# A two-layer linear-attention and routed-FFN kernel: the reciprocal denominators reach all features through DRAM instead of a TensorE broadcast, with fewer two-column matmuls and another order of instructions

## Chip, cores and metric

The kernel runs on one core of one Trainium2 chip. Its time is the device time of one execution in microseconds; the number quoted is the median of several runs. Besides the runs there is one profiled execution, and every duration below that is read from a view is from that one.

The five engines are called by their short names: PE is TensorE (PEld its weight loads), DVE is VectorE, ACT is ScalarE, POOL is GpSimd, SP is SyncE, which only issues DMAs here.

## What is computed

One token matrix x (2048 tokens, 512 features, bf16) passes four residual steps: attention A, routed FFN B, A again, B again, each on a layer-normalised x. The weights are the same in both rounds.

```
A: q, k, v = layernorm(x) @ wqkv            # 32 heads of 16 features
   pq, pk = phi(q), phi(k)                  # phi(t) = (t+1 if t>0 else exp(t)) + 1e-6
   kv = sum over tokens of pk^T v           # 16 x 16 per head
   z  = sum over tokens of pk               # 16 per head
   o  = (pq @ kv) / (pq . z + 1e-6)         # one denominator per token and head
   x  = x + o @ wo
B: r = layernorm(x) @ w_r; pick the one token with the largest r
   y = (silu(xs @ w_gate) * (xs @ w_up)) @ w_down * sigmoid(r)   # for this token alone
   x = x + layernorm(x); the picked token also gets + y
```

So there are 2048 x 32 denominators per layer, and each is needed on the 16 features of its head.

## The kernel before, in words

**Layout.** x lies in SBUF as 16 tiles of 128 tokens (`x_tok`), the normalised x both so (`xn_tok`) and transposed with features on partitions (`xnT`, one buffer per layer). Features come in four chunks m of 128, tokens for q and for the denominators in four groups tg of 512.

**Stages of a layer.** `kv_tile` computes keys and values of a token tile (four accumulating 128x512 matmuls each; L591, or L601 where a value tile carries router columns) and adds the tile's pk^T v, with a column of ones for z, into two PSUM banks reserved for it (L620). `q_group` computes the transposed queries of 512 tokens, one bank for each chunk (L681). Both apply phi in three steps on three engines: ACT takes exp from PSUM into a ring buffer `Eb` (L527), POOL clips it at 1 (L529), DVE combines it with the matmul's result (L531); only then is the bank free. `kv_out` then folds the per-head kv into wo: Mw = kv @ wo, four 128x512 matrices (L658), evicted on ACT and DVE (L663, L666).

**The division.** `den_group` handles 512 tokens. Four matmuls with z as weights (L779) give the denominators, one partition for each 4 features, so 32 partitions for each chunk, 128 in all; a head's value is there four times. ACT takes 1/d as exp(-ln(d)) into `rden` (L784, L786). To bring the value from 32 partitions to the 128 of its chunk, four matmuls with a 0/1 matrix `sel` (L809) copy it into four PSUM banks, and four DVE instructions multiply `pqT` in place by them (L814). `out_tile` then computes pq @ Mw for a token tile (L836; six tiles of layer 1 add x by an identity matmul, L839), DVE adds the residual and sums the row (L859), ACT squares and sums (L865).

**Narrow matmuls.** The router value r is linear in x, so it is built from its parts rather than from the new x: a matmul of only 2 columns with the same weights follows its wide one (`mm_keep`, L519: it reuses the loaded weights). The 2 columns are the high and low bf16 half of a vector. They go along with the output tiles of both layers (128 of them), with the layer-0 value tiles 4 to 15 (48) and the Mw products (8); for tiles 0 to 3 they stand alone (L754, 16).

**Between the layers.** `ln_mid` forms the statistics of both normalisations for groups of 2 or 4 tiles, POOL normalises (L718) and SP issues a DMA transpose for each tile (L409). Router and FFN of the first B run amid the keys and values of layer 1: layer 1 computes k and v for x without the picked token's y, and `coupling` repairs that by a rank-2 correction (L1094, L1114), a patch of one `xnT` column and of one x row on POOL (`x_patch`, L1136). `x2_explicit` (L931) updates six x tiles on POOL. At the end `final_group` normalises for the output (L1172, L1176) and SP stores it; the second B runs as a serial tail, with the token's column gathered through a register-held index (L975).

**Order.** Every operation is added once to a list with its reads and writes; ORDER, a list of operation numbers written out in the file, fixes the sequence for each engine, SP's DMA issues among them, and BANKS the PSUM bank of each buffer: six banks (0 to 5) serve everything but the kv sums. Engines run their sequence in order; semaphores are derived from reads and writes, and a buffer that takes over a bank waits for all users of the one before. All DMAs of SP go through one queue.

Of the kernel before, what the change touches and what calls it, by code (L numbers as in the profile page):

```python
# [7 lines left out]
ALU = mybir.AluOpType  # L8
# [3 lines left out]
P = 128  # L12
S_TOK = 2048
# [12 lines left out]
0 11 30 1 58 15 2 16 25 17 36 7 54 14 26 29 24 23 35 37 27 3 56 4 13 21 22 19 18 32 28 31 20 55 10 33 12 34 5  # L26
51 67 6 53 8 60 57 9 68 61 69 62 59 70 63 71 52 64 65 72 66 88 73 152 86 76 159 153 74 154 77 87 160 89 163 75
97 78 90 161 155 79 156 91 164 83 92 80 84 157 41 162 93 81 85 158 38 165 82 94 177 98 95 39 99 166 42 40 178
96 43 100 44 45 101 173 167 102 272 103 168 174 46 170 169 104 184 171 110 106 105 180 108 185 175 111 109 191
119 107 181 176 112 182 172 113 192 187 120 114 143 115 179 183 188 194 117 116 130 189 186 121 195 284 118  # L30
190 196 198 122 47 123 124 201 199 125 197 126 193 202 205 131 132 128 127 144 133 219 141 134 203 206 48 135
129 212 220 136 200 204 221 213 223 137 142 222 145 207 146 355 49 230 224 139 147 138 50 273 150 208 226 231
140 148 237 227 214 149 209 228 233 215 238 274 229 216 151 234 275 235 247 217 236 296 248 210 249 336 244
337 250 211 334 320 245 333 218 332 240 335 225 241 251 242 232 252 261 243 288 285 262 286 239 289 304 263
287 290 246 264 305 258 291 297 306 253 259 280 298 307 321 299 254 281 322 265 282 323 255 283 256 276 266
257 268 277 260 278 269 292 279 270 316 293 271 267 294 317 328 339 338 295 318 358 329 341 422 359 319 300
330 423 356 340 331 324 360 357 424 361 325 365 301 326 362 308 302 363 312 303 309 327 342 310 313 364 516
343 314 311 517 348 346 315 344 349 350 347 345 469 352 351 470 425 353 354 471 427 375 518 428 372 426 376
366 418 373 377 369 367 399 374 429 368 395 370 472 401 396 378 439 474 402 371 400 473 403 430 404 475 405
# [38 lines left out]

class Op:
    __slots__ = ("idx", "eng", "fn", "est", "prio", "deps", "is_dma", "nbytes", "kind", "sem", "val", "pos",  # L80
                 "has_dependents", "name", "banks", "known", "waits", "occ", "pre", "pre_deps")


class Sched:
# [1231 lines left out]
```

## Time and profile before

| what | value |
|---|---|
| median of 3 runs | 173.48 us (173.47 to 174.39) |
| the profiled execution | 172.91 us |
| its span, first to last instruction | 170.7 us |
| busy PE / DVE / ACT / POOL | 155.0 / 130.3 / 113.7 / 72.8 us |
| instructions in the span | 3500 |
| DMA | 15.80 MB in 23183 packets |
| granted TensorE clock | full up to 158 us, about half in the tail |

Rows are of four kinds. In the windows view a row is a stretch of time: busy time and number of instructions of PE, PEld, DVE, ACT and POOL, then the granted clock, the DMA engines' share and GB/s. In the groups, a row is a source line, engine, operation, output and inputs with shapes and count; then the busy time in us, the mean ns of one, and the idle time of the engine before them with what ended it. In the timeline a row is a start, a duration, an engine and an operation, merged when alike; the bracket is the engine's idle time before it and what ended that. In the DMA issues the last number is the median time from issue to landing. Consecutive instructions of PE and of DVE overlap in their rows, so a group's busy time is more than the engine's time for it: start-to-start distances tell that.

### The profile page before, as it was taken

The numbers are of one execution on the slowest core, as the hardware profiler recorded it, in microseconds if no ns is written. First come the engines' busy times: TensorE is split into PE (matmuls) and PEld (weight loads), VectorE is DVE, ScalarE is ACT, GpSimd is POOL, SyncE is SP. The second block draws the span as 40 slices with busy tenths as digits, with TensorE's granted clock in tenths as the row PEclk, the third lists the DMA queues.
The fourth block names the chain that finished last, engine by engine and source line by source line (L and its number), as shares of the span: only waits on it lengthen the run. The fifth ranks groups of instructions, "written<-read, shape, count | busy, mean of one in ns | idle before, by whom it ended". The sixth has DMA issues, their size and how long they took to land.

```text
span 170.7 us, 3500 instructions
## 1 busy us (share of the span) xinstructions
PE 155.0 (91%) x1332; PEld 73.0 (43%) x1148; DVE 130.3 (76%) x426; ACT 113.7 (67%) x293; POOL 72.8 (43%) x123
## 2 busy tenths in 40 slices
PE   7889999999999778999999898999999898997184
PEld 2335344445544222433344365667444233332073
DVE  6698998351669899999999662254698999999921
ACT  3476557744867786789779461764678669888920
POOL 4043776931655410242694689240576320153000
PEclk9999999999999999999999999999999999999855
DMA  5999433349995000033055430000000000031430
GB/s 133 344 312 255 83 75 62 63 70 340 352 381 213 4 0 0 0 61 67 0 103 109 95 67 0 4 0 4 0 2 0 0 4 0 0 123 61 184 127 0
DMA packets 23183, 15.80 MB, mean 93 GB/s; under 512 B 15616, under 2 KB 21632, under 8 KB 23040
## 3 DMA queue, kind: packets, MB, share of 16 engines
q1 hardware_dynamic: 23168, 15.60, 32.6%
q8 instruction: 9, 0.15, 0.4%
q14 instruction: 6, 0.05, 0.1%
HBM read 9.83 MB, written 2.10 MB: 70 GB/s over the span
## 4 chain that ended last, share of the span: by engine, by line
PE 58%; DVE 28%; DMA 6%; POOL 2%; ACT 2%; issue 1%; SPq 0%
PE ps L591 17%; PE ps L681 13%; PE ps L836 9%; DVE pqT L814 7%; PE ps L601 7%; DVE x_tok L859 5%; PE ps L620 4%; DMA x_tok<-in_A_x_dram 4%; DVE pqT L531 3%; DMA xnT<-xn_tok 3%; PE ps L1021 3%; DVE pk L531 2%; DVE st L725 2%; PE ps L1047 2%; DVE xn_tok L1176 1%
## 5 line engine op out<-in xcount | busy, mean ns | idle before, releaser
L529 POOL TENSOR_SCALAR Eb<-Eb 128x512 bf16<-128x512 bf16 x64 | 38.9, 612 | 45.7 <-ACT Eb L527 38.2
L591 PE MATMUL ps<-wqkv,xnT 128*128 128x512 bf16 x208 | 50.0, 379 | 1.2 <-DVE pk L531 0.5
L527 ACT ACTIVATE Eb<-ps 128x512 bf16<-128x512 f32 x64 | 37.6, 596 | 19.9 <-PE ps L591 9.9
L836 PE MATMUL ps<-Mw,pqT 128*128 128x512 bf16 x128 | 32.7, 377 | 1.5 <-DVE pqT L814 0.6
L681 PE MATMUL ps<-xnT,wqkv 128*128 128x512 bf16 x128 | 30.6, 380 | 1.3 <-DVE pqT L814 0.8
L531 DVE SCALAR_TENSOR_TENSOR pk<-ps,Eb 128x512 bf16<-128x512 f32 x32 | 21.6, 683 | 12.3 <-POOL Eb L529 12.3
L591 PEld LDWEIGHTS ps<-wqkv,xnT 128*128 128x128 bf16 x208 | 18.2, 97 | 21.6 <-DVE pk L531 0.9
L610 ACT ACTIVATE va<-ps 128x512 bf16<-128x512 f32 x32 | 18.8, 595 | 12.4 <-PE ps L519 4.3
L531 DVE SCALAR_TENSOR_TENSOR pqT<-ps,Eb 128x512 bf16<-128x512 f32 x32 | 21.2, 686 | 5.4 <-POOL Eb L529 5.2
L836 PEld LDWEIGHTS ps<-Mw,pqT 128*128 128x128 bf16 x128 | 12.3, 96 | 21.4 <-issue 1.8
L519 PE MATMUL ps<-mr_hl,pqT 128*128 128x2 bf16 x128 | 21.1, 165 | 0.0
L814 DVE TENSOR_TENSOR pqT<-pqT,ps 128x512 bf16<-128x512 bf16 x32 | 20.1, 682 | 0.7 <-PE ps L809 0.6
L865 ACT ACTIVATE junk<-x_tok 128x512 bf16<-128x512 bf16 x26 | 16.1, 620 | 4.2 <-DVE x_tok L859 3.9
L718 POOL TENSOR_SCALAR xn_tok<-x_tok,stat,nms 128x512 bf16<-128x512 bf16 x16 | 12.1, 768 | 15.3 <-DVE nms L901 11.3
L681 PEld LDWEIGHTS ps<-xnT,wqkv 128*128 128x128 bf16 x128 | 11.5, 97 | 15.2 <-DVE pqT L814 1.4
L601 PE MATMUL ps<-wqkv,xnT 128*128 128x512 bf16 x48 | 13.2, 377 | 0.3 <-DMA xnT<-xn_tok 0.3
L620 PE MATMUL ps<-va,pk 128*128 128x129 bf16 x128 | 12.0, 221 | 0.0
L725 DVE BATCH_NORM_STATS2 st<-x_tok 128x6 f32<-128x512 bf16 x16 | 10.3, 675 | 1.6 <-DMA x_tok<-in_A_x_dram 1.6
L859 DVE SCALAR_TENSOR_TENSOR x_tok<-x_tok,ps 128x512 bf16<-128x512 bf16 x16 | 10.7, 680 | 0.3 <-PE ps L519 0.2
L620 PEld LDWEIGHTS ps<-va,pk 128*128 128x128 bf16 x128 | 9.0, 99 | 4.6
L718 POOL TENSOR_SCALAR xn_tok<-x_tok,rs,nms 128x512 bf16<-128x512 bf16 x12 | 9.6, 806 | 2.2 <-DVE nms L738 1.9
L1176 POOL TENSOR_SCALAR xn_tok<-x_tok,us,stat 128x512 bf16<-128x512 bf16 x6 | 4.6, 774 | 13.6 <-DVE rt L1158 10.9
(207 smaller groups left out, 205.7 us busy)
## 6 DMA issues: line engine op xcount, KB each, us to landing
out_dram<-xn_tok SPq DMA_DIRECT2D x8, 256.0 KB, 2.1
wu<-in_B_w_up_dram SPq DMA_DIRECT2D x2, 896.0 KB, 9.4
wd<-in_B_w_down_dram SPq DMA_DIRECT2D x2, 896.0 KB, 9.6
wg<-in_B_w_gate_dram SPq DMA_DIRECT2D x2, 896.0 KB, 11.1
wqkv<-in_A_wqkv_dram SPq DMA_DIRECT2D x3, 512.0 KB, 7.1
x_tok<-in_A_x_dram SPq DMA_DIRECT2D x1, 1024.0 KB, 11.8
x_tok<-in_A_x_dram SPq DMA_DIRECT2D x2, 256.0 KB, 4.8
x_tok<-in_A_x_dram SPq DMA_DIRECT2D x1, 512.0 KB, 6.1
```

Of the source, the lines that this page charges most:

```text
L519: ins = e.matmul(out_ap, lhsT, rhs, start=start, stop=stop, skip_group_check=True).ins
L527: A("act", lambda e: e.activation(Eb[:, i, :], src(), ACTF.Exp), reads=[b, "table"], writes=[f"E{i}"], est=600, name=name + "E")
L529: A("pool", lambda e: e.tensor_scalar(Eb[:, i, :], Eb[:, i, :], 1.0, 0.0, op0=ALU.min, op1=ALU.max), reads=[f"E{i}"], writes=[f"E{i}"], es ...
L531: return A("dve", lambda e: e.scalar_tensor_tensor(out=dst, in0=src(), scalar=1e-6, in1=Eb[:, i, :], op0=ALU.max, op1=ALU.add), reads=[b, ...
L591: ins = e.matmul(B(b), xT[:, c, t * P:(t + 1) * P], wqkv[:, c, lo:lo + D], start=(c == 0), stop=(c == NC_D - 1))
L601: e.matmul(B(vb), xT[:, c, t * P:(t + 1) * P], wqkv[:, c, 2 * D:3 * D], start=(c == 0), stop=(c == NC_D - 1))
L620: ins = e.matmul(views[m], pk[:, i, m * P:(m + 1) * P], va[:, i, m * 129:(m + 1) * 129], start=(first and m in (0, 3)), stop=False, skip_g ...
L681: ins = e.matmul(B(qb), wqkv[:, c, qc * P:(qc + 1) * P], xnT[L][:, c, tg * 512:(tg + 1) * 512], start=(c == 0), stop=(c == NC_D - 1))
L718: A("pool", lambda e: e.tensor_scalar(xn_tok[:, t, :], x_tok[:, t, :], scale[:, t:t + 1], nbias[:, t:t + 1], op0=ALU.mult, op1=ALU.add), r ...
L814: A("dve", (lambda e, m=m, bb=bb: e.tensor_tensor(pqT[:, m, cols], pqT[:, m, cols], B(bb), ALU.mult)), reads=[bb, f"pq{tg}_{m}"], writes=[ ...
L836: e.matmul(B(ob), w, Mw[:, m, :], start=(m == 0), stop=(m == NC_D - 1 and not xb))
L859: A("dve", lambda e: e.scalar_tensor_tensor(out=x_tok[:, t, :], in0=x_tok[:, t, :], scalar=scal, in1=B(ob), op0=ALU.mult, op1=ALU.add, acc ...
```

## The change

- **Denominators.** For all eight groups, `den_group` no longer uses the `sel` matmuls. SP writes `rden` to a DRAM buffer, each of its 128 rows four times (512 rows of 1 KB, 512 KB), and after that has landed reads it back with the 512 rows as features (`rb_sb`, two buffers). DVE multiplies per token tile, all four chunks in one instruction of 128 x 512 bf16 with both inputs in SBUF; four such per group as before.
- **Router columns.** For tiles 0 to 7 the router's 2-column matmuls of layer 0 (value tiles 4 to 7, the lone ones of tiles 0 to 3, output tiles 0 to 7) are dropped. In their place 2-column matmuls follow layer 1's value matmuls of these tiles, into one bank held from the first to the reduction `Mrtx`; `router_mid` scales it.
- **kv banks.** The four kv products lie two and two in their banks, not three and one.
- **First router.** The picked row is copied on POOL (`B0xg`) and gathered from there; the statistics are summed by a matmul over all 4 x 16 columns and one reduction (as bf16 halves, in the second router in fp32). In the second router TensorE loads the index register when the index is there, and its matmuls wait for the rest; the sum `B1tot` stands ahead of the gather. `index` takes register values without another copy.
- **Rank-2 rows.** Key and value rows are computed in half-rows of 256, on four groups of columns.
- **Order.** ORDER and BANKS are new throughout. On SP: the loads of x, wk and wr come first, the weight loads for B stand between the transposes of tiles 15, 14 and 13; the new DMAs stand, in layer 0, as write 0, write 1, read 0, write 2, read 1, read 2, write 3, transposes of tiles 2 and 3, read 3; in layer 1 as write 0, write 1, read 0, read 1, write 2, write 3, read 2, read 3. On PE, in both layers the q matmuls of groups 2 and 3 stand behind the first denominators and ahead of the first output tile.

The diff, cut to its core:

```diff
-604 524 581 491 421 596 398 448 587 417 492 467 582 449 597 493 450 494 451 584 583 495 588 452 496 525 530
...
+249 289 254 294 276 243 255 295 25 250 256 281 290 257 282 264 291 285 335 336 283 296 355 286 284 301 356 292
...
+        RD = ()
+        RT = tuple(range(8))
+        RM = tuple(t for t in range(4, NT) if t not in RD + RT)
+        RS = tuple(t for t in range(4) if t not in RD + RT)
...
+        def index(e, reg, n):
+            return nc.s_assert_within(e.snap(reg, donate=True), 0, n - 1,
+                                      skip_runtime_bounds_check_because="built from max_index results alone")
...
-            if L == 0 and t in RM:
+            if L == 1 and t in RT:
+                if "b" not in rtb:
+                    rtb["b"] = bank()
+                rb = rtb["b"]
+
+                def vmr(e):
+                    ins = None
+                    for c in range(NC_D):
+                        e.matmul(B(vb), xT[:, c, t * P:(t + 1) * P], wqkv[:, c, 2 * D:3 * D], start=(c == 0),
+                                 stop=(c == NC_D - 1))
+                        ins = mm_keep(e, B(rb)[:, 2 * t:2 * t + 2], xT[:, c, t * P:(t + 1) * P], wrc_hl[:, c, :],
+                                      c == 0, c == NC_D - 1)
+                    return ins
+                A("pe", vmr, reads=[f"T{L}_{t}", "wv", "wrc_h", "wrc_l"], writes=[vb, f"rx{t}"], hold=[rb],
+                  est=864 + KEEP, name=f"A{L}v{t}")
+            elif L == 0 and t in RM:
...
-        DMAB = ()
+        DMAB = ((0, 0), (0, 1), (0, 2), (0, 3), (1, 0), (1, 1), (1, 2), (1, 3))
+        rd_dram = [nc.dram_tensor(f"rd_scr{i}", [NC_D * P, 512], BF).ap() for i in range(len(DMAB))]
 
         def den_group(L, tg):
             db = bank()
...
               reads=[f"lden{j}"], writes=[f"rden{j}"], est=629, name=f"A{L}rden{tg}")
             if (L, tg) in DMAB:
                 i = dctr[1] % 2
+                scr_d = rd_dram[dctr[1]]
                 dctr[1] += 1
-                row = 2 * NC_D * 512
-                for m in range(NC_D):
-                    src = bass.AP(rden, 32 * m * 1024 + j * 512, [[1024, 32], [0, 4], [1, 512]])
-                    dst = bass.AP(rb_sb, (i * NC_D + m) * 512, [[4 * row, 32], [row, 4], [1, 512]])
-                    DMA("sp", dst, src, [f"rb{i}_{m}"], TB * 1.25, f"A{L}rb{tg}_{m}", reads=[f"rden{j}"])
-                for m in range(0, NC_D, 2):
-                    pr = slice(m, m + 2)
-                    A("dve", (lambda e, pr=pr: e.tensor_tensor(pqT[:, pr, cols], pqT[:, pr, cols], rb_sb[:, i, pr, :],
-                                                               ALU.mult)),
-                      reads=[f"rb{i}_{m}", f"rb{i}_{m + 1}", f"pq{tg}_{m}", f"pq{tg}_{m + 1}"],
-                      writes=[f"pq{tg}_{m}", f"pq{tg}_{m + 1}"], est=690, name=f"A{L}qd{tg}_{m}")
+                DMA("sp", scr_d.rearrange("(q s) n -> q s n", s=4), rden[:, j, :].unsqueeze(1).to_broadcast([P, 4, 512]),
+                    [f"rd{L}{tg}"], 4 * TB, f"A{L}rw{tg}", reads=[f"rden{j}"])
+                DMA("sp", rb_sb[:, i, :, :], scr_d.rearrange("(m p) n -> p m n", p=P), [f"rb{i}"], 4 * TB,
+                    f"A{L}rb{tg}", reads=[f"rd{L}{tg}"])
+                for t in range(4 * tg, 4 * tg + 4):
+                    tc = slice(t * P, (t + 1) * P)
+                    rc = slice((t - 4 * tg) * P, (t - 4 * tg + 1) * P)
+                    A("dve", (lambda e, tc=tc, rc=rc: e.tensor_tensor(pqT[:, :, tc], pqT[:, :, tc], rb_sb[:, i, :, rc],
+                                                                      ALU.mult)),
+                      reads=[f"rb{i}"] + [f"pq{tg}_{m}" for m in range(NC_D)], writes=[f"pqd{t}"], est=420,
+                      name=f"A{L}qd{t}t")
                 return
...
-            if (L, k) not in rbanks:
+            keep = L == 1 or t not in RT
+            if keep and (L, k) not in rbanks:
                 rbanks[(L, k)] = bank() if L == 0 else bank(("ka", "kb")[[g[0] for g in FG].index(k) % 2])
-            rb = rbanks[(L, k)]
+            rb = rbanks[(L, k)] if keep else None
             q = t - k
 
             def womm(e):
                 ins = None
                 for m in range(NC_D):
                     w = pqT[:, m, t * P:(t + 1) * P]
-                    e.matmul(B(ob), w, Mw[:, m, :], start=(m == 0), stop=(m == NC_D - 1 and not xb))
-                    ins = mm_keep(e, B(rb)[:, 2 * q:2 * q + 2], w, mr_hl[:, m, :], m == 0, m == NC_D - 1)
+                    ins = e.matmul(B(ob), w, Mw[:, m, :], start=(m == 0), stop=(m == NC_D - 1 and not xb))
+                    if keep:
+                        ins = mm_keep(e, B(rb)[:, 2 * q:2 * q + 2], w, mr_hl[:, m, :], m == 0, m == NC_D - 1)
                 if xb:
...
+            if (L, tg) in DMAB:
+                pqr = pqr + [f"pqd{t}"]
...
+            if k in RT:
+                tiny_act(ics[:, sl], l2[:, sl], ACTF.Exp, [f"l2_{k}"], [f"ics{k}"], f"Mic{k}", scale=0.5)
+            else:
+                router_mid(ts)
+
+        def router_mid(ts):
+            sl = slice(ts[0], ts[-1] + 1)
+            k = ts[0]
+            n = len(ts)
+            u_ = usx[:, sl] if set(ts) & set(XB) else us1[:, sl]
+            if k in RT:
+                tt(rt[:, sl], rt[:, sl], ics[:, sl], ALU.mult, [f"rt{k}", f"ics{k}"], [f"rt{k}"], f"Mro{k}")
+            else:
+                rb = rbanks[(0, k)]
+                A("dve", lambda e: e.tensor_reduce(
+                    rt[:, sl], B(rb)[:, 0:2 * n].rearrange("p (m k) -> p m k", k=2), AX.X, ALU.add),
+                  reads=[f"rr0_{t}" for t in ts], writes=[f"rt{k}"], hold=[rb], est=160, name=f"Mrt{k}")
+                tt(rt[:, sl], rt[:, sl], aw[:, sl], ALU.add, [f"rt{k}"] + [f"aw{t}" for t in ts], [f"rt{k}"], f"Mro{k}")
             tt(r_bf[:, sl], rt[:, sl], rs1[:, sl], ALU.mult, [f"rt{k}", f"rs1_{k}"], [f"r{k}"], f"rbf0_{k}")
...
             gb = bank()
 
+            gregs = {}
+            if L == 0:
+                def load_t(e):
+                    e.reg_load(reg_t, idxu[0:1, 1:2])
+                    regs["t"] = index(e, reg_t, NT)
+                    return e.tensor_copy(xg[:], x_tok[:, bass.ds(regs["t"], 1), :].rearrange("p a d -> p (a d)"))
+                A("pool", load_t, reads=["idxu1"] + [f"x{t}" for t in range(NT)], writes=["xg", "regt"], est=1250,
+                  name="B0xg")
+
+            def gather_reg(e):
+                e.reg_load(reg_pe, idxu[0:1, 1:2])
+                gregs["t"] = index(e, reg_pe, NT)
+
             def gather(e):
-                e.reg_load(reg_pe, idxu[0:1, 1:2])
-                tv = e.snap(reg_pe)
                 ins = None
                 for c in range(NC_D):
-                    ins = e.matmul(B(gb)[:, c:c + 1],
-                                   x_tok[:, bass.ds(tv, 1), c * P:(c + 1) * P].rearrange("p a d -> p (a d)"),
-                                   ohp_bf[:, 0:1], start=True, stop=True)
+                    src = xg[:, c * P:(c + 1) * P] if L == 0 else x_tok[
+                        :, bass.ds(gregs["t"], 1), c * P:(c + 1) * P].rearrange("p a d -> p (a d)")
+                    ins = e.matmul(B(gb)[:, c:c + 1], src, ohp_bf[:, 0:1], start=True, stop=True)
                 return ins
-            A("pe", gather, reads=["idxu1", "ohp_bf"] + [f"x{t}" for t in range(NT)], writes=[gb], est=650,
...
-                                       start=True, stop=True),
-              reads=["part_h", "part_l", "ones_bf", "part0"], writes=[tb], est=30, name=tag + "tot")
...
+            else:
+                A("pe", lambda e: e.matmul(B(tb)[:, 0:nw], ones_mat[:, :], pv, start=True, stop=True),
+                  reads=["prod16", "ones_mat"], writes=[tb], est=280, name=tag + "tot")
+                tv_ = lambda: B(tb)[:, 0:nw].rearrange("p (k t) -> p k t", t=NT)
+                ax = AX.X
+            small(lambda e: e.tensor_reduce(tots[:, 0:nr], tv_(), ax, ALU.add), [tb], ["tots"], tag + "tots",
...
+            HD = D // 2
+
             def rows(e):
                 ins = None
                 for c in range(NC_D):
-                    for r, lo in ((0, D), (32, 2 * D)):
-                        ins = e.matmul(B(kb2)[r:r + 2, :], xcol2[:, c, :], wqkv[:, c, lo:lo + D], start=(c == 0),
+                    for r, lo in ((0, D), (32, D + HD), (64, 2 * D), (96, 2 * D + HD)):
+                        ins = e.matmul(B(kb2)[r:r + 2, 0:HD], xcol2[:, c, :], wqkv[:, c, lo:lo + HD], start=(c == 0),
                                        stop=(c == NC_D - 1))
...
         for t in range(NT):
             kv_tile(1, t, kva1, kvb1)
+        nrt = len(RT)
+        A("dve", lambda e: e.tensor_reduce(rt[:, 0:nrt], B(rtb["b"])[:, 0:2 * nrt].rearrange("p (m k) -> p m k", k=2),
+                                           AX.X, ALU.add), reads=[f"rx{t}" for t in RT],
+          writes=[f"rt{g[0]}" for g in MG if g[0] in RT], hold=[rtb["b"]], est=180, name="Mrtx")
+        for g in MG:
+            if g[0] in RT:
+                router_mid(g)
```

## The prediction

> **What bounds it now.** I read the windows view by stage first, because shares over the whole span mix stages.
>
> ```profile
> 8.00:53.00 45.00, 44.22 (x312) 20.84 (x263) 32.08 (x80) 29.08 (x61) 25.25 (x38) 1.00 0.74 209
> 53.00:63.00 10.00, 7.88 (x57) 2.82 (x50) 9.32 (x21) 8.36 (x16) 3.64 (x6) 1.00 0.07 25
> 75.00:90.00 15.00, 14.93 (x95) 6.22 (x75) 14.97 (x61) 12.55 (x44) 9.81 (x14) 1.00 0.30 61
> 119.00:137.00 18.00, 17.33 (x96) 6.96 (x88) 14.77 (x28) 13.11 (x24) 10.23 (x16) 1.00 0.00 0
> 137.00:159.00 22.00, 19.02 (x154) 7.01 (x90) 21.92 (x79) 18.83 (x60) 5.19 (x7) 1.00 0.10 39
> ```
>
> After the stretch and its length come the busy times of PE, its weight loads, DVE, ACT and POOL. TensorE bounds the kernel to 53 us. At 53 to 63 it idles 2 us, VectorE does not. To 90 both are full; to 137 TensorE binds again. At 137 to 159 VectorE is full (21.9 of 22) and TensorE waits 3 us. What follows is a serial tail.
>
> Next the timeline around the first division by the denominators, TensorE's rows:
>
> ```profile
> 55.82 0.39 PE L809 MATMUL ps<-rden,sel 32*128 32x512 bf16 x4
> 57.01 1.90 PE L681 MATMUL ps<-xnT,wqkv 128*128 128x512 bf16 x8 [0.80 <-DVE pqT L814]
> ...
> 61.88 0.39 PE L809 MATMUL ps<-rden,sel 32*128 32x512 bf16 x4 [0.27 <-DVE mr_f L668]
> 62.76 0.39 PE L836 MATMUL ps<-Mw,pqT 128*128 128x512 bf16 x1 [0.48 <-DVE mr_hl L546]
> 62.98 0.17 PE L519 MATMUL ps<-mr_hl,pqT 128*128 128x2 bf16 x1
> 63.01 0.38 PE L836 MATMUL ps<-Mw,pqT 128*128 128x512 bf16 x1
> ```
>
> The broadcast L809 fills four of six banks; the projection behind it waits 0.80 us until L814 has emptied one. L836 to L836 with a narrow L519 between takes 0.24 us, while eight L681 take 1.90, 0.217 each: a narrow matmul costs 0.024 us, not the 0.165 of its row.
>
> The page's group of the multiply, and three timeline rows of DVE and POOL:
>
> ```profile
> L814 DVE TENSOR_TENSOR pqT<-pqT,ps 128x512 bf16<-128x512 bf16 x32 | 20.1, 682 | 0.7 <-PE ps L809 0.6
> ```
> ```profile
> 79.39 0.15 DVE L546 SCALAR_TENSOR_TENSOR r_bf<-rt,stat 128x2 bf16<-128x2 f32 x1
> 79.53 0.59 DVE L546 SCALAR_TENSOR_TENSOR r_bf<-rt,stat 128x2 bf16<-128x2 f32 x1
> ```
> ```profile
> 79.49 0.61 POOL L529 TENSOR_SCALAR Eb<-Eb 128x512 bf16<-128x512 bf16 x1 [2.66 <-ACT l L691]
> ```
>
> The same two-column product, both inputs in SBUF, takes 0.15 us and then 0.59, ending with the POOL instruction it overlaps. I return to that.
>
> **The change, part by part.**
>
> *The broadcast goes.* L809 occupies 0.33 us of TensorE (in the timeline 76.54 to the next issue at 76.87): 8 x 0.33 = 2.6 us, mostly where TensorE binds. With it go the bank waits: 0.80 at 57, 0.27 at 61.9, and 0.7 at 67 to 68.
>
> *The multiply.* L814 reads PSUM; four in a row take 2.41 us, 0.60 each. The new one has 512 bf16 elements too, all in SBUF. No row shows a bf16 tensor-tensor from SBUF. Upper bound: 0.60, as now. Lower bound: the Trainium skill ("VectorE: DVE Perf Modes", The perf-mode tier table) has a bf16 SBUF tensor-tensor at two elements a cycle and one with a PSUM operand at one; 1224 ns against 2293 at 2048 elements gives, with L814's 682 as the slow end, about 0.42 us, or 0.34 start to start (rows overlap by 0.08). The nearest row, L714's bf16 SBUF tensor-scalar, has 405 ns. I take 0.34: 32 x 0.26 = 8.3 us less VectorE.
>
> *A rule against the change.* The Trainium skill ("SBUF — State Buffer", Who interferes with whom) says a VectorE instruction with two SBUF inputs and a GpSimd one that reads SBUF exclude each other for the whole instruction. L814 is exempt now, with one input in PSUM; its successor is not. The 0.59 row agrees. By the rule: about 8 multiplies of layer 0 run where POOL is 65% busy (9.81 of 15), the 16 of layer 1 where it is 24% busy (5.19 of 22); half an instruction's wait is 0.35 us, so 8 x 0.65 x 0.35 + 16 x 0.24 x 0.35 = 3.2 us. The saving is 8.3 without the rule and 5.1 with it. I use 5.1.
>
> *The round trip.* Each group writes 512 KB and reads 512 KB back, both in SP's one queue, the read waiting for the write. The nearest row is the 256 KB store:
>
> ```profile
> out_dram<-xn_tok SPq DMA_DIRECT2D x8, 256.0 KB, 2.1
> wqkv<-in_A_wqkv_dram SPq DMA_DIRECT2D x3, 512.0 KB, 7.1
> ```
>
> At the page's best rates (340 to 380 GB/s) another 256 KB add 0.75: 2.9 us a leg. Upper end: the 512 KB wqkv load's 7.1 us, but that stood in a queue of some 4 MB. I take 2.9 and keep 7.1. Is it covered? I counted through the new ORDER. Layer 0, from den0: lden and rden end at 1.9 us (0.69 + 0.63 after 0.3 matmul and 0.3 wait), so data is back at 1.9 + 5.8 + 0.3 for two issues = 8.0. TensorE meanwhile has eight projection groups (8 x 0.864), two more denominators, kvT and four M's: 8.8 us, then the last two Mw evictions on ACT, so the first output tile could start at 10.4 anyway. Slack 2.4 us. Layer 1 has the same eight groups and more: about 11 us. Second groups have 10 us, third and fourth 9 or more. So the legs cost nothing up to about 4.1 us each; without that cover each group would cost its 6 us. SP's in-order queue: rb3 stands behind transposes T2 and T3 and ahead of T0, T1; what waits for rb3 (tile 15) comes about 4 us of TensorE work after T3 is needed. The weight loads (5.4 MB, 36.9 to 53.8 us now) stand earlier in the new list, behind T15; at 359 GB/s they end about 47, before the first write near 51.
>
> *Narrow matmuls.* 200 (L519 128 + 48 + 8, L754 16) become 168: 32 x 0.024 = 0.8 us (L754 too: four take 0.10, 33.35 to 33.45). The 32 of tiles 0 to 7 now stand in layer 1's value matmuls, where TensorE also binds. A PSUM bank is held for them through those eight tiles: nothing if banks suffice, 0.5 us if not; I take 0.2.
>
> *Coupling rows.* L1094's eight 512-wide matmuls (0.96 us) become sixteen 256-wide in four column groups: about 0.5. Gain 0.4, TensorE-bound.
>
> *Order.* Ahead of layer 1's output, Mx27 (0.77) and Cxpatch (1.15, row of L1136) now stand on POOL amid the q groups, ahead of q2_0's minimum; 1.9 us of delay against roughly two banks' slack (0.86 us each): 0 to 1.5 us, I take 0.7. B0xg adds a POOL copy (0.6 us) in front of queued minimums, while Cregs shrinks: even. Start-up DMAs are reordered: between -0.5 and +0.5, zero.
>
> *Tail.* The index reaches idxu at 161.16, the gather starts at 162.12 because of the register load; that stays. The sum tot (0.2) and its reduction (0.17) no longer follow the gather, and one 0.36 us L1176 leaves the argmax chain: 0.6 us less.
>
> **Sum**, against the profiled execution: 172.91 us, of which the span is 170.7 and 2.2 lie around it.
> - To the first output tile (62.76): two L809 0.66, the wait at 57 0.80, 32 narrow matmuls 0.8 (16 of layer 0's value tiles' 48, 16 of L754), and the idle between 58.75 and 62.76, 2.0 now, shrinks to the 1.6 of the Mw evictions above (10.4 - 8.8): -2.7.
> - From there to layer 1's q (119.4): two L809 0.66, bank waits 0.7, rows 0.4, less 0.3 for k2 waiting on T2 and 0.2 for the bank: -1.3. (Its 32 narrow ones fewer in the output tiles are the 32 more in the value tiles.)
> - q to its first output tile (137.18): three denominators move in front (3 x 0.33 = 1.0) and the POOL delay 0.7 is added; one L809 and the waits around it (0.47 and 0.38) go: +0.5.
> - Output to argmax (137.18 to 158.93, 21.75 us): TensorE needs 16 x 0.97 + 6 x 0.216 = 16.8, plus 2.4 after the last tile = 19.2. VectorE's work falls by 12 x 0.26 and three L531 (1.8) moved in front, to 16.9, plus 1.3 port waits. TensorE becomes the bound: -2.5, I take -2.2.
> - Tail -0.6.
>
> Together -6.3: 166.6. The median of the runs (173.48) lies 0.57 above the profiled execution, so 167.2.
>
> **Rivals.**
> (A) As summed, 167.2, own range 164.5 to 171: chance 0.55.
> (B) The released banks also close TensorE's other gaps. From 7.9 to 137 its work at 0.217 us a wide matmul leaves some 8 us unfilled; another 4 closed gives 163.2. For: six banks were often all taken. Against: many gaps follow ACT and POOL. 0.07.
> (C) The multiply doesn't pack two elements, or POOL's lock eats the saving. The output stage stays VectorE-bound (+2.2) and layer 0 loses about 2: 171.4. For: the 0.59 row. 0.14.
> (D) Slower: the legs are slow. Place: first group of each layer, TensorE idle at the first output tile. Below 4.1 us a leg it costs nothing; above, each microsecond counts twice per layer, 4 in all. At 4.1 + 6.3/4 = 5.7 us all of the gain is eaten; beyond that the kernel is slower. At 6 us: +7.6, 174.8; at the 7.1 of wqkv's row 179. For: written and read back through one queue, rows of 1 KB, and a write with a repeated source that no row shows. Against: the stores' 2.1 us. 0.24.
> That the change doesn't do what it says holds only for the narrow matmuls: 16% go.
>
> **Numbers.** Range 164 to 175: B and the upper half of D (0.07 + 0.12) lie outside, about 0.2. Under 0.5% a measurement of this kernel can't tell from no change. Faster: A, B and most of C, 0.71; same 0.06; slower: D and a rest of C, 0.23.
>
> **What would show it.** The multiply at 0.42 us, or 0.68 (C). 2.9 us to landing for the new DMAs, or 5.7 and more with TensorE waiting on rb_sb before the first output tile (D). The first output tile at 60 to 61. VectorE under 20 of 22 us in layer 1's output stage. A TensorE wait near q2_0's minimum. I am wrong if TensorE's idle time before 137 grows.

## The result, and the profile after

| | before | after |
|---|---|---|
| median of 4 runs each | 173.47 us (172.76 to 174.39) | 167.53 us (165.48 to 168.85) |
| ratio, 95% interval | | 0.957 (0.947 to 0.966) |
| the profiled execution, its span | 172.91, 170.7 us | 166.57, 164.4 us |
| busy PE / DVE / ACT / POOL | 155.0 / 130.3 / 113.7 / 72.8 us | 150.0 / 121.7 / 112.4 / 75.0 us |
| DMA | 15.80 MB | 24.20 MB |

By the medians the kernel became 3.4% faster; 167.2 us was predicted. The ratio, 4.3%, leaves out executions more than 1.5% above the kernel's fastest, here 168.49 and 168.85 at a mean granted clock of 0.95 against 0.97, but experiment 4 gives reason to count them as the kernel's own.

The two traces can be laid side by side at four events which both have. All times are us from the start of the span:

| event | before | after | change of the stretch | predicted |
|---|---|---|---|---|
| first output tile of layer 0 | 62.76 | 60.82 | -1.94 | -2.7 |
| first output tile of layer 1 | 137.18 | 134.14 | -1.10 | -1.3 + 0.5 |
| argmax of the second router | 158.93 | 153.03 | -2.86 | -2.2 |
| end of the span | 170.7 | 164.4 | -0.40 | -0.6 |

The total, -6.3, is the predicted one, but the four stretches miss by 0.2 to 0.8 us each and cancel: that it fits so closely is luck. The windows of the changed kernel, cut at the same kinds of places:

```profile
8.00:53.00 45.00, 43.11 (x284) 20.37 (x250) 32.62 (x82) 28.92 (x61) 25.84 (x41) 1.00 0.73 214
53.00:63.00 10.00, 8.40 (x49) 3.43 (x43) 8.78 (x21) 6.78 (x13) 4.07 (x7) 1.00 0.81 259
75.00:90.00 15.00, 15.00 (x113) 6.14 (x69) 11.55 (x53) 13.08 (x49) 9.21 (x13) 1.00 0.36 72
119.00:137.00 18.00, 16.82 (x106) 6.91 (x91) 15.29 (x36) 14.19 (x27) 10.58 (x17) 1.00 0.48 163
134.14:153.03 18.89, 16.90 (x134) 6.35 (x70) 17.08 (x78) 15.27 (x54) 5.01 (x6) 1.00 0.47 157
```

The last row is layer 1's output stage up to the argmax: it lasts 18.89 us where it lasted 21.75, and VectorE is busy for 17.08 of them. TensorE, 16.90, runs in it without a gap to 151.04: it is the bound there now, up to its last tile. In the row 75 to 90 TensorE is full while VectorE fell from 14.97 to 11.55. But the first two rows do not show the closed gaps that the sum counted on: 1.9 us are open from 8 to 53 (0.8 before), 1.6 from 53 to 63 (2.1 before).

Groups and DMA issues of the page, for the multiply and the round trip:

```profile
L858 DVE TENSOR_TENSOR pqT<-pqT,rb_sb 128x512 bf16<-128x512 bf16 x32 | 12.9, 439 | 0.0
```
```profile
rd_scr<-rden SPq DMA_DIRECT2D x8, 512.0 KB, 3.4
rb_sb<-rd_scr SPq DMA_DIRECT2D x8, 512.0 KB, 4.3
out_dram<-xn_tok SPq DMA_DIRECT2D x8, 256.0 KB, 2.4
```

The multiply takes 439 ns instead of 682, and 0.0 says that VectorE never stood idle for its data. The trip takes 3.4 + 4.3 us, against 2.9 + 2.9 predicted. The waits that TensorE has left are new ones, in its timeline:

```profile
22.96 4.48 PE L607 MATMUL ps<-wqkv,xnT 128*128 128x512 bf16 x20 [1.64 <-DMA xnT<-xn_tok]
...
60.82 2.76 PE L897 MATMUL ps<-Mw,pqT 128*128 128x512 bf16 x12 [1.47 <-DVE pqT L858]
...
105.63 1.02 PE L607 MATMUL ps<-wqkv,xnT 128*128 128x512 bf16 x4 [1.48 <-DMA xnT<-xn_tok]
...
134.14 0.39 PE L897 MATMUL ps<-Mw,pqT 128*128 128x512 bf16 x1 [0.75 <-DVE tot L561]
```

Two of the four wait for a transposed tile, two for the first multiply or for what stands in front of it on VectorE. None waits for the trip through DRAM.

### The profile page after: what moved, and what is told of

Read it like the earlier page. It is cut to its first block, busy times and chain, and to the rows that moved or that the text cites. A ratio compares the mean times of both kernels' runs of the same rounds, so it can differ in the third digit from the quotient of the medians.

```text
span 164.4 us, 3413 instructions
## 1 busy us (share of the span) xinstructions
PE 150.0 (91%) x1277; PEld 71.9 (44%) x1109; DVE 121.7 (74%) x422; ACT 112.4 (68%) x296; POOL 75.0 (46%) x123
## 2 busy tenths in 40 slices
DMA packets 31632, 24.20 MB, mean 147 GB/s; under 512 B 15872, under 2 KB 30080, under 8 KB 31488
## 4 chain that ended last, share of the span: by engine, by line
PE 52%; DVE 18%; DMA 11%; POOL 8%; ACT 7%; issue 2%; SPq 1%; POOLq 0%
PE ps L897 17%; PE ps L712 11%; DMA xnT<-xn_tok 9%; PE ps L607 9%; PE ps L621 5%; POOL Eb L544 4%; ACT Eb L542 3%; DVE pk L546 3%; POOL xn_tok L749 3%; PE ps L1120 3%; DVE pqT L546 2%; DVE st L756 2%; DMA x_tok<-in_A_x_dram 2%; PE ps L651 2%; PE ps L1146 2%
## 5 line engine op out<-in xcount | busy, mean ns | idle before, releaser
L607 PE MATMUL ps<-wqkv,xnT 128*128 128x512 bf16 x192 | 46.5, 379 | 3.4 <-DMA xnT<-xn_tok 3.3
L897 PE MATMUL ps<-Mw,pqT 128*128 128x512 bf16 x128 | 31.6, 377 | 2.2 <-DVE pqT L858 1.5
L607 PEld LDWEIGHTS ps<-wqkv,xnT 128*128 128x128 bf16 x192 | 16.9, 97 | 21.0 <-issue 1.9
L749 POOL TENSOR_SCALAR xn_tok<-x_tok,stat,nms 128x512 bf16<-128x512 bf16 x16 | 12.8, 808 | 14.3 <-DVE nms L965 7.6
L534 PE MATMUL ps<-mr_hl,pqT 128*128 128x2 bf16 x96 | 15.8, 164 | 0.0
L858 DVE TENSOR_TENSOR pqT<-pqT,rb_sb 128x512 bf16<-128x512 bf16 x32 | 12.9, 439 | 0.0
L749 POOL TENSOR_SCALAR xn_tok<-x_tok,rs,nms 128x512 bf16<-128x512 bf16 x12 | 10.0, 838 | 3.1 <-DVE nms L769 1.9
L534 PE MATMUL ps<-wrc_hl,xnT 128*128 128x2 bf16 x64 | 10.5, 164 | 0.0
```

The costliest lines, as they stand in the source:

```text
L534: ins = e.matmul(out_ap, lhsT, rhs, start=start, stop=stop, skip_group_check=True).ins
L607: ins = e.matmul(B(b), xT[:, c, t * P:(t + 1) * P], wqkv[:, c, lo:lo + D], start=(c == 0), stop=(c == NC_D - 1))
L749: A("pool", lambda e: e.tensor_scalar(xn_tok[:, t, :], x_tok[:, t, :], scale[:, t:t + 1], nbias[:, t:t + 1], op0=ALU.mult, op1=ALU.add), r ...
L897: ins = e.matmul(B(ob), w, Mw[:, m, :], start=(m == 0), stop=(m == NC_D - 1 and not xb))
```

## The experiments

Five questions were open: whether the two-elements-a-cycle multiply carries the gain (rival C), how near the trip is to deciding (rival D), where the closed waits went, whether TensorE's work still sets the time, and what the change's parts are worth alone. Medians are of 4 runs unless said otherwise; each ratio is to the kernel before on the same chip.

**1. The multiply without its packing.** The same product in the instruction form with a scalar. Everything else stays.

```diff
-e.tensor_tensor(pqT[:, :, tc], pqT[:, :, tc], rb_sb[:, i, :, rc], ALU.mult)
+e.scalar_tensor_tensor(out=pqT[:, :, tc], in0=pqT[:, :, tc], scalar=1.0,
+                       in1=rb_sb[:, i, :, rc], op0=ALU.mult, op1=ALU.mult)
```

> The changed kernel (profiled execution 166.57 us) with the 32 multiplies by the reciprocals written as a scalar-tensor-tensor operation instead of a tensor-tensor one; same operands, same result. Both theories expect the multiply itself at about 0.68 us instead of 0.42 (0.60 instead of 0.34 start to start), which is 8.3 us more VectorE work. Theory 1 (the prediction's rival C, that VectorE bounds the output stages as soon as the multiply costs what it cost before): VectorE is busy 17.1 of 18.9 us in layer 1's output stage and gets 4.0 more, so at least 2.2 us there, and about 2 in layer 0: 170.5 to 171.5. Theory 2 (the gain is TensorE's removed work, and VectorE had slack): within 1 us of 166.6.

Measured: ratio 0.990 (0.985 to 0.994), from the three of 10 executions that kept a mean granted clock of 0.97, 170.6 to 171.7 us. The other seven took 173.2 to 175.7 at 0.94 to 0.965, so the median of all ten, 173.29, shows no gain at all. The group in its page:

```profile
L858 DVE SCALAR_TENSOR_TENSOR pqT<-pqT,rb_sb 128x512 bf16<-128x512 bf16 x32 | 20.9, 688 | 0.0
```

The instruction is back at 688 ns, VectorE's group at 20.9 us. Where the clock held in both kernels, 166.0 us on average (166.57 and 165.48) became 171.3, some 5 us, and of the gain of 4.3% one of 1.0% is left. The forecast for rival C, 171.4, was the right price of this part: with the trip in place and the broadcast gone, most of the gain still hangs on the fast multiply.

**2. A third leg for the trip.** A copy from DRAM to DRAM between write and read.

```diff
+DMA("sp", cp_dram[dctr[1] - 1], scr_d, [f"rc{L}{tg}"], ..., reads=[f"rd{L}{tg}"])
-DMA("sp", rb_sb[:, i, :, :], scr_d...., reads=[f"rd{L}{tg}"])
+DMA("sp", rb_sb[:, i, :, :], cp_dram[dctr[1] - 1]...., reads=[f"rc{L}{tg}"])
```

> The changed kernel with one more leg in every round trip: write to DRAM, copy to a second DRAM buffer, read back; same result. A leg takes about 3.8 us. Theory 1 (the prediction's rival D: what counts is the sum of the legs, free up to 4.1 us a leg, then four times the excess): 7.7 + 3.8 = 11.5 us a trip is 5.75 a leg, so 4 x 1.65 = 6.6 us more: 173. Theory 2 (the queue counts too: the third and fourth writes stand in SP's order behind reads that now wait longer): a walk through the queue gives 2.9 us at the first output tile of layer 0 and 2.3 more at its later groups, 2.3 at the first of layer 1 and 4.2 more at its later groups, 11.7 in all: 178. Theory 3 (the trips are hidden deep under other work): under 168.

Measured: 194.67 us (192.35 to 198.91), ratio 1.114 (1.105 to 1.122), far above every expectation, the 178 of Theory 2 too. The copy took 4.6 us to land. In the view of waits a row gives the waiting and the awaited, the sum in us, how often and the longest:

```profile
DVE pqT L862 <- DMA rb_sb<-cp_scr: 25.2, 8, 4.2
```

All eight groups wait, 3.15 us each on average. The changed kernel's own trace shows why. Adding each read's issue time and its time to landing (3.8 to 4.5 us), the eight land at 59.3, 63.2, 66.3, 74.8, 132.4, 134.5, 140.3 and 142.8; the first multiplies that use them start at 60.3, 64.2, 66.6, 74.8, 133.6, 135.1, 141.8 and 144.4 (the sixth and the eighth lie inside rows of several, placed by 0.335 us each). No group has more than 1.6 us to spare. With a leg more, every group pays, and groups are chained: one that comes late holds TensorE, and with it the next denominators and the next trip; and SP's queue holds a later write behind an earlier read. So beyond the slack all eight groups wait, not two as in rival D. What a late microsecond costs in all can't be read from the 29 us by which the span grew (164.4 to 193.8), because the clock fell too: TensorE's busy time rose from 150.0 to 159.0 us though no matmul was added. The pages give the granted clock in 40 equal slices of the span, in tenths of full speed (9 is 90% or more), first the changed kernel's, then this one's:

```profile
PEclk9999999999999999999999999999999999999755
```
```profile
PEclk9999999999999589997999999589999979889955
```

Some 9 of the 29 us may be that, an estimate from the two busy times. The mechanism of rival D is real, and its threshold lies just above what the chip took.

**3. Tile 14 normalised ahead of the row copy.** The wait of 1.48 us at 105.63 traces back to POOL:

```profile
97.28 0.61 POOL L1052 COPY xg<-x_tok 128x512 bf16 x1 [1.66 <-DVE x2w L561]
97.85 0.61 POOL L544 TENSOR_SCALAR Eb<-Eb 128x512 bf16<-128x512 bf16 x1
98.45 0.81 POOL L1008 TENSOR_SCALAR x_tok<-x_tok,usx,nmrx 128x512 bf16<-128x512 bf16 x1
...
100.58 0.77 POOL L749 TENSOR_SCALAR xn_tok<-x_tok,stat,nms 128x512 bf16<-128x512 bf16 x1
```

B0xg (L1052) needs the router's index; POOL stands 1.66 us for it, and behind it stands the normalisation (L749) whose transpose TensorE then awaits. The edit moves one number of ORDER:

```diff
-... 550 638 708 649 624 ... 715 627 562 709 ...
+... 550 638 562 708 649 624 ... 715 627 709 ...
```

> The changed kernel with one POOL instruction moved: the normalisation of tile 14 for layer 1 stands ahead of the copy of the selected token's tile, which waits for the index, instead of behind it and two other instructions; same result. Theory 1 (the TensorE wait of 1.48 us at 104.15 for tile 14's transpose is the price of the copy's place in POOL's queue, which the prediction put at nothing): tile 14 is normalised some 5 us earlier, the wait goes, 165.1 to 165.5. Theory 2 (another wait takes its place at once, since VectorE and ACT are as late): within 0.5 of 166.6.

Measured: 164.04 us (163.53 to 165.82), ratio 0.950 (0.942 to 0.958). The wait is gone; from layer 0's first output tile to layer 1's first q matmul the trace takes 52.26 us (60.22 to 112.48) against 53.86 (60.82 to 114.68), 1.6 less, and 0.6 more came from the first 60 us, where the wait near 22 happened to be 0.40 instead of 1.64; that is why the time lies below the 165.1 expected at best. This is the fastest kernel here, and the kernels below marked "with 3" contain this edit.

**4. The changed kernel again.** Its four runs lay at 165.5, 166.6, 168.5 and 168.9. The kernel ran unedited once more, beside experiment 7.

> The changed kernel itself, nothing edited, for its spread: its four times lie at 165.5, 166.6, 168.5 and 168.9. Theory 1 (TensorE's wait of 1.5 us at 104, in the midst of one-column matmuls, sometimes lets its granted clock fall, as patch_late's trace shows at 102 to 114 us): both groups of times again, the longer ones at a mean granted clock near 0.95 and the shorter near 0.97, while xn14_first, without that wait, had 163.5 to 165.8 at 0.97 in all four. Theory 2 (chance): one group of times.

Measured: 168.66 us (6 runs, 167.71 to 171.81), ratio 0.974 (0.969 to 0.980). First the changed kernel's first profile, then the repeat's, in the same three windows; the ninth number of the row, ahead of DMA share and GB/s, is the granted clock:

```profile
102.00:106.00 4.00, 2.52 (x56) 1.81 (x54) 1.47 (x6) 1.37 (x4) 0.62 (x1) 1.00 0.44 37
106.00:110.00 4.00, 4.00 (x78) 2.75 (x76) 1.35 (x7) 2.39 (x7) 1.94 (x3) 1.00 0.00 0
110.00:114.00 4.00, 4.00 (x83) 3.14 (x79) 2.31 (x11) 1.42 (x4) 0.84 (x3) 1.00 0.01 4
```
```profile
102.00:106.00 4.00, 2.41 (x47) 1.59 (x44) 1.19 (x5) 1.09 (x4) 0.61 (x1) 0.92 0.45 37
106.00:110.00 4.00, 4.00 (x56) 2.19 (x54) 1.11 (x6) 1.21 (x4) 1.37 (x2) 0.50 0.00 0
110.00:114.00 4.00, 4.00 (x78) 2.92 (x77) 1.52 (x3) 1.18 (x3) 1.41 (x3) 0.73 0.01 4
```

The same wait (1.48 and 1.59 us) is followed once by the full clock and once by half of it for four microseconds and 0.73 for four more. That explains a second time, some 2 us higher, and experiment 3, which has no such wait, shows no such drop (four executions at 0.97). But both groups of times were expected, and here all six lie in the upper one, at 0.94 to 0.96: of the changed kernel's ten executions two kept the clock, so the lower time is the rarer one. Why one execution loses the clock and another doesn't, no run shows; nor does a lower mean clock always cost time: in experiment 6 two executions at 0.96 took 166.0 and 166.7 us, one at 0.975 took 166.9. The Trainium skill ("TensorE: Matmul & The Clock Gate", Part 1) has the clock fall after an idle window of about 3.4 us; here it fell behind 1.6 us amid one-column matmuls, and not behind 1.5 in another execution. Several kernels of this study fell into it, which blurs their comparison by about 2 us.

**5. Patch and Mx27 behind the last minimum of q.** The prediction charged 0.7 us to their new place on POOL.

```diff
-... 861 747 818 ... 45 776 897 ... 828 837 ...
+... 861 818 ... 45 897 ... 828 747 776 837 ...
```

> The changed kernel with two POOL instructions (the explicit update of tile 7, 0.77 us, and the patch of the selected token, 1.16) moved from between the q groups of layer 1 to behind the last of them; same result. Theory 1 (the prediction's step: they delay the following minimums and so cost 0.7): 165.9. Theory 2 (TensorE shows no wait there, 24 projection matmuls in 5.35 us, so banks cover the delay): within 0.3 of 166.6.

Measured: 167.45 us (166.78 to 167.78), ratio 0.965 (0.960 to 0.971), with the clock of experiment 4 down in its profile (0.50 at 106 to 110). The local reading is free of that: from the start of q to the first output tile 19.93 us, against 19.46. The place that I charged cost nothing, the late one costs 0.5, for this reason (DVE, then POOL):

```profile
134.74 0.61 DVE L561 SCALAR_TENSOR_TENSOR mr_hl<-mr_f,ones_mat 128x4 bf16<-128x4 f32 x1
...
134.18 1.15 POOL L1236 TENSOR_TENSOR x_tok<-x_tok,ypatch 128x512 bf16 x1
```

A product of four columns, 0.15 us in the changed kernel, lasts until the POOL instruction ends.

**6. POOL kept busy under the multiplies** (with 3). Twelve instructions on a tile of their own behind q's last minimum; they add nothing to the result.

```diff
+for i in range(12):
+    A("pool", lambda e: e.tensor_scalar(dum[:], zeros[:], 1.0, 0.0, op0=ALU.min, op1=ALU.max), ...)
```

> The kernel of xn14_first (164.0 us) with twelve more POOL instructions of 0.61 us, on a tile of their own that nobody reads, in the stretch where POOL idles while VectorE makes layer 1's first eight multiplies; same result. Theory 1 (a VectorE instruction with two SBUF inputs and a POOL instruction exclude each other, as the rule of the prediction says; the changed kernel paid little for it only because POOL happens to idle there): the eight multiplies go from 0.42 to 0.7 to 0.95 us, the first output tile comes 1 to 2 us later, 165 to 166.5. Theory 2 (they share the port at little cost): 0.42 to 0.5 us, 164.0.

Measured: 166.44 us (166.00 to 166.85), ratio 0.962 (0.957 to 0.966), 2.4 us above experiment 3. Six multiplies in a row in the changed kernel, then here, and what POOL does meanwhile:

```profile
134.07 2.09 DVE L858 TENSOR_TENSOR pqT<-pqT,rb_sb 128x512 bf16<-128x512 bf16 x6
```
```profile
133.66 4.15 DVE L859 TENSOR_TENSOR pqT<-pqT,rb_sb 128x512 bf16<-128x512 bf16 x6
...
130.83 8.89 POOL L1373 TENSOR_SCALAR dum<-zeros 128x512 bf16<-128x512 bf16 x12
```

0.35 us each become 0.69, which agrees with the exclusion of the prediction's rule: where both engines run, each multiply waits for about half a POOL instruction. In the changed kernel they seldom do: 32 x (439 - 418) ns = 0.7 us over all multiplies, 418 being the median.

**7. The first output tile of layer 0** (with 3). Mw's matmuls earlier and the first multiply ahead of a feature map, to open the wait at 60.82.

```diff
-... 312 359 343 327 ... 316 347 461 321 348 318 ... 322 341 349 342 350 320 323 346 351 363 ...
+... 312 359 343 345 327 ... 316 347 341 461 346 342 321 348 349 350 351 318 ... 322 363 320 323 ...
```

> The kernel of xn14_first (164.0 us) with the products Mw of layer 0 and their evictions moved up, as in m_early, layer 1 left alone, and the multiply of the first output tile moved ahead of one feature map on VectorE, behind which it stood in m_early (59.66 to 60.27 us) although its data were there; same result. Theory 1 (the first output tile waited for VectorE's order, not for the reciprocals): it comes 0.6 to 1.0 us earlier than in xn14_first (60.22), 163.0 to 163.5 in all. Theory 2 (the reciprocals land no earlier than that, and VectorE now stands before them with the feature map behind it): 164 or more, with a wait of VectorE for rb_sb.

Measured: 165.53 us (6 runs, 164.41 to 166.24), ratio 0.957 (0.952 to 0.961), no gain over experiment 3; beside experiment 4 on the same chip it is 3.1 us faster, most likely by the edit of 3 and the clock that it keeps. The tile started at 60.27, no earlier than the 60.22 of experiment 3: two q groups ahead of it waited 0.22 and 0.23 us, and the multiply lasted 0.64:

```profile
59.58 0.64 DVE L858 TENSOR_TENSOR pqT<-pqT,rb_sb 128x512 bf16<-128x512 bf16 x1
```

The same move for both layers, with layer 1's last denominators moved back too, gave 169.04 us (6 runs), ratio 0.971 (0.966 to 0.977).

> The kernel of xn14_first (164.0 us) with the products Mw and their evictions, which the first output tile of each layer waits for, moved up between the last q groups of the layer, and in layer 1 the last denominator moved behind the second output tile; same result. Theory 1 (the first output tile waits for the Mw evictions and what follows from them on VectorE, not for the reciprocals, as the prediction's working of 10.4 against 8.0 us has it): TensorE's waits of 1.46 us at 58.8 and 0.2 + 0.2 + 0.75 at 129 to 132 shrink until the reciprocals' landing binds (some 1.0 us earlier in layer 0, 1.2 in layer 1): 161.8 to 162.5. Theory 2 (the round trip is as late as the evictions: no slack): 163.5 to 164.5, and VectorE's rows show a wait for rb_sb.

The later denominators sent the trips of groups 2 and 3 late, TensorE stood for a multiply in the output stage (1.07 us at 144.99), and the clock fell at 133 to 137. Layer 0's first tile came at 60.74, later than in experiment 3: VectorE had taken a feature map first, with the data already there.

**8. Denominators computed twice** (with 3). It repeats the eight groups' four matmuls, 2.6 us of TensorE, and gives the same result.

```diff
-for m in range(NC_D):
+for m in [0, 1, 2, 3] * 2:
```

> The kernel of xn14_first (164.0 us) with every group's four denominator matmuls issued twice into the same bank; same result. It puts back on TensorE what the change took off it with the broadcasts, 8 x 0.33 = 2.6 us, and nothing else. Theory 1 (TensorE binds nearly everywhere in the changed kernel, so work removed from it is time): 166.0 to 166.6. Theory 2 (VectorE, ACT and the trips set the stages with the denominators, and the removed broadcasts brought little): 164.0 to 165.0.

Measured: 165.99 us (164.67 to 166.52), ratio 0.957 (0.950 to 0.963): 1.95 us above experiment 3 by the medians, but 1.2 us by the ratios, since the two ran on different chips, and the intervals of the ratios overlap. So of 2.6 us added, about half to three quarters seem to come out at the end. That speaks for TensorE setting the time at most of these places; the worth of the broadcasts, which stood elsewhere, is not fixed more closely by it.

**9. Parts alone.** The trips in the kernel before, at the places of the broadcasts, nothing else changed:

> The kernel before with one part of the change alone: every group's reciprocals go through DRAM and the multiplies read SBUF by token tile, each at the place in the old order where the old ones stood; same result. A trip takes 2.3 us to the reciprocals and 8 more. In the old order the first multiply follows its denominator by 3 to 8 us. Theory 1 (the order is what hides the trips, and every one of the eight counts, as third_leg showed): some 5 + 0 + 4 + 0 us in layer 0 and 3 + 3 + 5 + 0 in layer 1 of waiting, less 4 saved: 183 to 192. Theory 2 (the prediction's rival D: only the first group of each layer is exposed): 5 + 3 - 4, so 176 to 179. Theory 3 (the trip pays by itself): under 172.

Measured: 196.23 us (194.36 to 197.56), ratio 1.130 (1.121 to 1.139), above the 183 to 192 of the nearest expectation. TensorE's timeline there has

```profile
66.20 0.62 PE L781 MATMUL ps<-pqT,Zr 128*32 128x512 bf16 x4 [8.00 <-DVE pqT L532]
```

In the old order nothing lies between denominators and output tile, so TensorE stands for the whole trip. Behind the wait its granted clock was 0.50 for six microseconds, and its busy time was 159.0 us against 155.0 with the broadcasts, so a part of the loss is the clock's. The new order with the broadcast back in (with 3; `rden` in four buffers):

> The new order with the old way to spread the reciprocals: TensorE broadcasts them into four PSUM banks and VectorE multiplies from PSUM, as before the change; the DMA trips are left out, and tile 14's normalisation stands ahead of the copy as in xn14_first (164.0 us). Same result. Theory 1 (the trip is the gain: slow_mul showed some 5 us for the slower multiply alone, and TensorE gets its 8 x 0.33 = 2.6 us back): 171 to 173, about the kernel before. Theory 2 (the new order is most of the gain, whichever way the reciprocals travel): 165 to 168.

Measured: 194.33 us (192.80 to 195.29), ratio 1.123 (1.115 to 1.131). It doesn't answer its question. I had put each group's broadcast and multiplies directly ahead of its output tiles, as its banks demand, and TensorE waited there:

```profile
PE ps L898 <- DVE pqT L875: 14.4, 7, 2.8
```

A worth of the trip alone, in an order fitted to each way, is not to be had from these two. As built here either half alone costs over 20 us, part of it by the clock in the second one too (TensorE busy for 161.5 us). That speaks for order and trip being one change; a better order around the broadcast was not tried. Last, the narrow matmuls of tiles 0 to 7 back at their old places (with 3):

> The kernel of xn14_first (164.0 us) with the old way for the router's columns of tiles 0 to 7: eight groups of four narrow matmuls in layer 0, and narrow matmuls in layer 0's output tiles, instead of those in layer 1's value tiles; no bank is held for them through layer 1. Same result. Theory 1 (the prediction's step: 32 narrow matmuls at 0.024 us each, less 0.2 for the bank): 164.6. Theory 2 (the eight groups carry their own weight loads and VectorE gets three reductions in its full stretch of 60 to 75 us): 165.5 or more. Theory 3: within 0.3 of 164.0.

Measured: 168.59 us (166.66 to 170.47), ratio 0.971 (0.964 to 0.978). Here the first trip landed late in the profiled execution, VectorE waited 0.84 us for it, TensorE 2.40, and then the clock fell to 0.57 for four microseconds:

```profile
62.00:66.00 4.00, 4.00 (x21) 1.37 (x10) 2.66 (x8) 0.98 (x4) 0.00 (x0) 0.57 0.69 239
```

How much of the 4.5 us above experiment 3 is the narrow matmuls' own, priced at 0.8, can't be separated from that. One execution, at a mean clock of 0.974, took 166.66 us, still 2.6 above; its trace was not kept.

## Why the prediction was right, and where not

**The main steps held.** The broadcast's 2.6 us left the engine that mostly binds (experiment 8, for about half of it or more). The closeness of 167.53 to 167.2 says less: the median lies between two groups of times, and the repeat gave 168.66; the profiled execution, 166.57 against 166.6, fits because the misses of the stretches cancel. The multiply starts every 0.335 us against the 0.34 taken, and VectorE's work in the output stage made room for TensorE (row 134.14 to 153.03, experiment 1). TensorE's need there was put at 16.8 and is 16.9.

**"Port waits 3.2": 0.7.** The lock is seen in experiment 6. The prediction took POOL's share of a stage as the chance of meeting it; the multiplies met POOL more seldom than that, perhaps because both engines follow the same tiles, which no run tested. The output stage gave -2.86 and not -2.2 for another reason: by the prediction's own sum TensorE bounds it at 19.2 us, which is -2.55, and 0.35 of that was held back; what follows TensorE's last tile then took 2.0 us instead of 2.4.

**Closed waits: repaid.** To layer 1's first output tile the sum counted on net 1.5 us less idle time. TensorE's idle time there went from 7.26 to 7.53 us, the sign that I had named for being wrong. The waits named did close (0.80 at 57, 0.27, those at 67 to 68, 0.47, 0.38). In their place came 1.64 at 22.96, 1.47 at 60.82, 1.48 at 105.63 and 0.75 at 134.14. The step that failed most plainly is "B0xg ... while Cregs shrinks: even": the copy was costed by its 0.6 us and not by the 1.66 us that POOL stands for its index, nor by tile 14 behind it; experiment 3 gives it 1.6 us, and it brings the risk of half clock besides.

**Unpriced work made up for it.** TensorE's busy time before layer 1's first tile fell by 3.3 us, not by the 1.85 that the sum's terms of work come to. Two reasons are in the rows: the gather of the first router, which the sum left out, took 0.79 us and takes 0.24; and two groups of denominators moved in front of that tile, not three (before, 129.59 and 136.40 already stood there), 0.33 us less. The remaining 0.6 us are not traced. The coupling rows, priced at 0.4, went from 1.03 us to 0.61.

**The legs: 3.4 and 4.3 us instead of 2.9 twice.** Still covered, but the slack of 2.4 us at layer 0's first multiply was in fact about 1.0. SP issued the read at 54.96, it landed 4.3 us later, near 59.3, and the multiply could run at once:

```profile
54.96 0.38 SPq L425 DMA_DIRECT2D rb_sb<-rd_scr  x1
```
```profile
59.67 0.68 DVE L546 SCALAR_TENSOR_TENSOR pqT<-ps,Eb 128x512 bf16<-128x512 f32 x1
60.27 0.16 DVE L561 SCALAR_TENSOR_TENSOR mr_hl<-mr_f,mr_hl 128x4 bf16<-128x4 f32 x1
60.34 1.43 DVE L858 TENSOR_TENSOR pqT<-pqT,rb_sb 128x512 bf16<-128x512 bf16 x4
```

It ran at 60.34, when VectorE had done what stands ahead of it. "Second groups have 10 us, third and fourth 9 or more" was no bad count of the cover; but the trips that it was held against, 6.1 us, took longer: from the end of `rden` to the read's landing 7.6 us for the first group, 9.3 for the second and 8.8 for the fourth, whose read stands on SP behind two transposes (write issued at 65.97, read at 70.75). Hence rival D's price, which let only the first group of each layer pay, was too low.

**Small ones.** Mx27 and Cxpatch: 0.7 taken, none found (experiment 5). Tail: the argmax chain gained 0.8 us to the gate matmuls, but four stores now stand in a row at 156.44 and land up to 4.7 us later; the last row's store waits for them and starts 0.6 us after its row is ready, so 0.4 and not 0.6 us remain. The worth of the narrow matmuls stays open.

## To carry to other kernels

In this kernel a detour through DRAM that takes work from the binding engine was free only as long as its landing lay ahead of the next use, and with chained groups each one paid for a late landing anew: count the slack for every group, not for the first. Cost a moved instruction by what it waits for and by what stands behind it in its queue, not by its own duration. Where two engines exclude each other, as in experiment 6, what matters is whether their instructions fall together, which shares of busy time do not tell.

## What was not expected of the hardware

- The clock fell after short waits of TensorE: to 0.50 after 1.59 us amid one-column matmuls, to 0.57 after 2.40 us, and not after 1.47 us at 60.82 or, in the first profile, after 1.48 us. Executions of the changed kernel that lost the clock were about 2 us longer.
- A product of four columns with both inputs in SBUF took 0.61 us beside a POOL instruction and 0.15 without one: the stretch follows POOL's instruction, not its own size.
- 512 KB from SBUF to DRAM with each row repeated four times landed after 3.4 us, the read back after 4.3, a copy from DRAM to DRAM after 4.6, beside 256 KB stores at 2.4.
